# Weight conversion in two VectorE passes, one operation for sum and inverse, pairs from unit 16: one attention and gated MLP kernel, replanned

## The chip, the cores and the metric

The kernel runs on one core of one Trainium2 chip. The metric is the device time of one execution in microseconds. The median of three runs of the kernel before is 406.76 us (406.49 to 407.43).

## The reference

Attention over 4 batches, 8 heads, 768 positions and 64 columns a head, followed by a gated MLP over the joined heads. A query sees the 8 first keys and the 96 latest; the bias is a slope per head times the distance.

```python
scores = q @ k.T / sqrt(64) - slope * dist          # kept: key < 8, or 0 <= rel < 96
a = exp(scores - max);  a = a / (sum(a) + 1e-9)
x = (a @ v) heads joined                            # [4, 768, 512]
h = gelu(x @ w_in);  u, v = h[:, :512], h[:, 512:]  # w_in float64
v_n = layernorm(v) * g_ln
v_s = w_sg @ v_n + b_sg                             # mixes the 768 positions
out = x + (u * v_s) @ w_out                         # w_out float64
```

## The kernel before, in words

**Units.** Attention is cut into 48 units: batch, then the third of the queries (256 rows, two tiles), then the pair of heads (four pairs). So units 0 to 11 are batch 0, 12 to 23 batch 1, and units 16 to 19 are the middle third of batch 1. For one unit the DMA queue loads q and k (`load_qk`, L1086, 380 KB) and v (`load_v`, L1093), TensorE makes 16 small score products (`score`, L1112), VectorE adds the bias and takes the largest (L1134, four per unit), ScalarE takes the exponential with its sum (L1139, four), the four sums get 1e-9 added on the engine that the plan chooses (ScalarE L1146, GpSimd L1148, VectorE L1150), VectorE inverts them (L1152), and GpSimd scales the four blocks (L1159). Then the weights are transposed. Units 0 to 15 (`TURNS`) do it on TensorE (L1220) with a copy out of PSUM (L1225). Later units do it by VectorE in 32x32 blocks (L1188), four DMAs to DRAM (`far<-tt`, L1196) and one back (`pt<-far`, L1200). Last TensorE multiplies by v (`weigh`, L1247): 24 products, then a score step, then 8 more that add to the same banks.

**Singles and pairs.** Up to unit 19 units are weighed one by one; from unit 20 (`PAIRS`, L121) two at a time, so 48 products, scores, 16 products, and the scores run one unit further ahead. Up to unit 19 (`DIRECT`, L119) `take` (L1333) copies the result to `xh` (L1345) and splits it from there into a high and a low part of x (L1357, L1363); from unit 20 `take_late` splits it straight from PSUM (L1320, L1324), the low part on VectorE.

**The MLP** works in split float: each operand is a high part rounded for TensorE plus the rest, and a product is three (L598, L599, L600). Per batch there are six v tiles (512 columns), and u, mix and out tiles (384 columns). Batch b's MLP runs beside batch b+1's attention. The last output is made from 28 instead of 32 block products (`Blocks`, L846).

**Weights.** `w_in` and `w_out` arrive as float64. `load_split` (L922) turns a piece into float32 by integer arithmetic: ScalarE scales the high word (L937), then VectorE makes three passes: shift left by 3 (L940), or-in the low word's top bits (L942), or-in the sign (L944). A copy (L947) and a difference (L949) make the two parts. There are 20 such pieces: four of 512 columns (the v half of `w_in`, needed by the first product of the MLP), eight of 256 (the u half), eight of 256 (`w_out`). `w_sg` is float32 and needs no conversion. `w_out`'s raw piece lies in a tile of the set `t`, its result in one of the set `diag`, four tiles each; the MLP's temporaries are in `t` too.

**The order.** Nothing is queued by hand. Each operation is entered with the engines that could do it and their modelled times (`op`), a due time is worked back from TensorE's list, and each due time gets a shift from the long string `SHIFTS`. `order` (L378) then plays the plan: each engine takes, by due time plus shift, the first operation that is ready and has room. The instructions are emitted in that order and each engine keeps it. TensorE stays within 40 operations of its own list. Before 29 us it fills planned gaps with products of zeros into a bank that is about to be used (`zeros` L534, `keep_on` L542).

```python
119 DIRECT = 20
121 PAIRS = 20
537 if not n or gap < IDLE or o.begin > ON_UNTIL: return 0
```

Of the kernel before, what the change touches and what calls it, by code (L numbers as in the profile page):

```python
# [1723 lines left out]
```

## Time and profile before

| | |
|---|---|
| median of 3 runs | 406.76 us |
| the profiled execution's own time | 408.85 us |
| its span, first to last instruction | 407.1 us |
| TensorE, VectorE, ScalarE, GpSimd busy | 97, 77, 56, 57% of the span |
| DMA | 68.78 MB, mean 169 GB/s |

The span is what the trace covers; 1.75 us of the profiled execution lie around it. The profiled execution is 2.09 us above the median. Busy TensorE is not TensorE at its peak: the ends of products are modelled, and products of zeros count as busy.

### The profile page before, as it was taken

Reading aid. Unit: us, or ns where it says so; the run is one execution under the profiler, and the core shown is the slowest. Engines: PE = TensorE matmul, PEld = TensorE weight load, DVE = VectorE, ACT = ScalarE, POOL = GpSimd, SP = SyncE. Lnnn points to the kernel's source line nnn. Section 1 sums busy time; section 2 is a strip of 40 time slices with the busy share of each in tenths; the row PEclk is TensorE's granted clock in tenths of the full one; section 3 lists DMA queues with packets and bytes.
Section 4 is the critical chain, followed back from the end, with each engine's and each line's share of the span. In section 5 each row is a group of like instructions: output and inputs, shape, how many; then the busy total and the mean of one; then the engine's idle time right before and its main releaser. Section 6 shows DMA issues by size and latency. Waiting matters only on the chain.

```text
span 407.1 us, 11302 instructions
## 1 busy us (share of the span) xinstructions
PE 395.3 (97%) x3980; PEld 358.5 (88%) x3980; DVE 312.0 (77%) x1041; ACT 226.1 (56%) x746; POOL 233.2 (57%) x395
## 2 busy tenths in 40 slices
PE   7989999999988999999999999999999999999994
PEld 4878778999977888999999898999999888999994
DVE  5897999999968889967766889957766668823782
ACT  5999999956637556544244575644245244533310
POOL 3766976673857566373455536354455244899640
PEclk9999999999999999999999999999999999999999
DMA  7866756148799696747778784746657521000004
GB/s 216 317 191 184 241 196 209 55 161 252 184 288 298 193 289 187 198 120 205 185 245 237 224 232 124 209 99 204 184 206 195 163 61 39 2 1 0 2 22 142
DMA packets 50368, 68.78 MB, mean 169 GB/s; under 512 B 5888, under 2 KB 34432, under 8 KB 50304
## 3 DMA queue, kind: packets, MB, share of 16 engines
q1 hardware_dynamic: 50304, 67.99, 56.2%
q8 instruction: 33, 0.54, 0.6%
q14 instruction: 31, 0.25, 0.2%
HBM read 49.61 MB, written 18.35 MB: 167 GB/s over the span
## 4 chain that ended last, share of the span: by engine, by line
PE 80%; DVE 8%; DMA 5%; SPq 2%; POOL 1%; issue 1%; ACT 0%; DVEq 0%; ACTq 0%
PE mm_ps L598 21%; PE mm_ps L600 20%; PE mm_ps L599 20%; PE av L1247 7%; PE s_ps L1112 6%; PE mm_ps L846 4%; PE tps L1220 3%; DMA qk<-in_qk_in_dram 3%; DMA far<-tt 2%; SPq L1196 1%; DVE p L1134 1%; POOL p L1159 1%; DMA v<-in_v_in_dram 1%; DVE tt L1188 1%; DVE win L949 1%
## 5 line engine op out<-in xcount | busy, mean ns | idle before, releaser
L1139 ACT ACTIVATE p<-p,pst 128x168 f32<-128x168 f32 (+1 forms) x192 | 81.2, 429 | 34.6 <-DVE pst L1134 32.6
L1159 POOL TENSOR_SCALAR p<-p,pst 128x168 f32<-128x168 f32 (+1 forms) x187 | 84.5, 469 | 24.0 <-DVE pst L1152 22.3
L598 PE MATMUL mm_ps<-wsg,z 128*128 128x384 f32 x192 | 64.9, 338 | 0.0
L600 PE MATMUL mm_ps<-wsg,z 128*128 128x384 f32 x192 | 64.2, 334 | 0.0
L599 PE MATMUL mm_ps<-wsg,z 128*128 128x384 f32 x192 | 64.2, 334 | 0.0
L1134 DVE CUSTOM_DVE_ANT_0 p<-s_ps,bias 128x168 f32<-128x168 f32 (+1 forms) x192 | 53.1, 317 | 6.0 <-PE s_ps L1112 4.0
L1247 PE MATMUL av<-pt,v 64*64 64x128 f32 (+1 forms) x1408 | 48.9, 250 | 1.9 <-DVE pst L1152 1.1
L1247 PEld LDWEIGHTS av<-pt,v 64*64 64x64 f32 x1408 | 40.6, 133 | 10.6 <-issue 3.8
L598 PE MATMUL mm_ps<-x,win 128*128 128x384 f32 x128 | 43.7, 342 | 0.0
L600 PE MATMUL mm_ps<-x,win 128*128 128x384 f32 x128 | 42.9, 335 | 0.2 <-DVE win L949 0.2
L599 PE MATMUL mm_ps<-x,win 128*128 128x384 f32 x128 | 42.8, 334 | 0.0
L1112 PE MATMUL s_ps<-qk 64*64 64x168 f32 (+1 forms) x768 | 38.7, 307 | 2.0 <-DMA qk<-in_qk_in_dram 2.0
L598 PE MATMUL mm_ps<-win,x 128*128 128x512 f32 x96 | 39.7, 413 | 0.0
L714 POOL TENSOR_TENSOR o<-o,x 128x384 f32<-128x384 f32 x24 | 24.3, 1016 | 25.4 <-DVE o L712 16.0
L1188 DVE STREAM_TRANSPOSE tt<-p 128x384 f32<-128x384 f32 (+1 forms) x64 | 33.4, 545 | 7.0 <-POOL p L1159 3.6
L600 PE MATMUL mm_ps<-win,x 128*128 128x512 f32 x96 | 37.7, 393 | 0.0
L599 PE MATMUL mm_ps<-win,x 128*128 128x512 f32 x96 | 37.7, 392 | 0.0
L1139 ACT ACTIVATION_READ_ACCUMULATOR p<-p,pst 128x1 f32 x192 | 37.5, 195 | 0.0
L598 PEld LDWEIGHTS mm_ps<-wsg,z 128*128 128x128 f32 x192 | 36.0, 188 | 1.1 <-issue 0.9
L1148 POOL TENSOR_SCALAR pst<-pst 128x4 f32<-128x4 f32 x38 | 9.9, 260 | 46.5 <-ACT p L1139 43.3
L600 PEld LDWEIGHTS mm_ps<-wsg,z 128*128 128x128 f32 x192 | 36.0, 188 | 0.1
L599 PEld LDWEIGHTS mm_ps<-wsg,z 128*128 128x128 f32 x192 | 36.0, 188 | 0.0
(148 smaller groups left out, 926.4 us busy)
## 6 DMA issues: line engine op xcount, KB each, us to landing
qk<-in_qk_in_dram SPq DMA_DIRECT2D x32, 380.0 KB, 4.2
far<-tt SPq DMA_DIRECT2D x96, 96.0 KB, 2.4
pt<-far SPq DMA_DIRECT2D x24, 384.0 KB, 4.6
v<-in_v_in_dram SPq DMA_DIRECT2D x32, 256.0 KB, 3.9
out_dram<-o SPq DMA_DIRECT2D x28, 192.0 KB, 2.8
qk<-in_qk_in_dram SPq DMA_DIRECT2D x15, 276.0 KB, 3.5
v<-in_v_in_dram SPq DMA_DIRECT2D x16, 192.0 KB, 3.2
far<-tt SPq DMA_DIRECT2D x32, 80.0 KB, 2.9
```

The source lines that it names most:

```text
L598: mm(ps.ap, ah, bh, start=(i == 0), stop=False)
L599: mm(ps.ap, ah, bl, start=False, stop=False)
L600: mm(ps.ap, al, bh, start=False, stop=(i == n - 1))
L714: lo = lambda eng: eng.tensor_tensor(o.ap, o.ap, xm[:, 1, :].bitcast(F32), ALU.add)
L846: mm(ps.ap, pa(h)[:, ms], pb(g), start=(first and k == n == 0), stop=True, skip_group_check=True)
L1112: nc.tensor.matmul(to, qk[rows, qc:qc + HQ], keys, start=True, stop=True)
L1134: nc.vector.tensor_tensor_reduce(out=p[:, g, 0:nk], in0=s_ps[h][:, i * W:i * W + nk], in1=bias[:, 2 * j + h, w0:w0 + nk], op0=ALU.add, op1 ...
L1139: op([on_act(nk, 0.225) + (lambda p=p, g=g, nk=nk, i=i: nc.scalar.activation(p[:, g, 0:nk], p[:, g, 0:nk], AF.Exp, bias=st[:, 0, i, g:g + ...
L1159: op([on_pool_ts(nk, -0.10) + (partial(scaled, lambda o, a, c: nc.gpsimd.tensor_scalar(o, a, c, 1.0, ALU.mult, ALU.mult)),),][:1 if n < TU ...
L1188: nc.vector.transpose(out, src.rearrange("p g (b j) -> p g b j", j=QB))
L1220: nc.tensor.transpose(tps[i][:, a * P:(a + 1) * P], pc[:, c:c + P], ident)
L1247: nc.tensor.matmul(to, v[rows, vc:vc + D], of, stop=True, skip_group_check=True, **kw)
```

## The change

- **Conversion.** The shift left and the sign no longer have passes of their own on VectorE. One pass multiplies the high word as a float by 0.0, which leaves its sign alone, in place in the raw piece, on GpSimd or on VectorE as the plan chooses (`SIGN` = 999 lets both be chosen). Then VectorE ors the low word's top bits into that, and a second VectorE pass shifts the scaled word left by 3 and ors it in.
- **Sum and inverse** are one operation of the plan: on VectorE the two instructions in a row, or on GpSimd an addition and a power of -1 (`POWER` = 0 lets both be chosen). ScalarE no longer takes part.
- **Pairs** and the direct split of x begin at unit 16 instead of 20 (`PAIRS`, `DIRECT`).
- **Tiles.** The set `diag` is gone, `t` has six tiles instead of four, and both tiles of a `w_out` piece come from `t`.
- **Zeros.** The first operation on a bank that is planned to begin between 5 and 9 us gets four products of zeros ahead of it if it had none (`WARM`).
- **Model and order.** The played plan adds 0.9 us once to the first DMA after 2.4 us (`STALL`), one rule of the order changes from 7.773 to 7.178, and all 62-base shifts are new.

```diff
-RULES = (7.773165816547267, 15.003852384881524, 0.25509251116156784)
+RULES = (7.177642220784175, 15.003852384881524, 0.25509251116156784)
 SHIFTS = (
...
-DIRECT = 20
+DIRECT = 16
-PAIRS = 20
+PAIRS = 16
-PLACES = {..., "pst": 2, "diag": 4, "tt": 1, ..., "t": 4, ...}
+PLACES = {..., "pst": 2, "tt": 1, ..., "t": 6, ...}
+STALL = 2.4, 0.9
+SIGN = 999
+LOW = 999
+POWER = 0
+WARM = 5.0, 9.0, 4
...
                     wire = max(wire, t + 1.3) + way[2]
+                    if t > STALL[0] and not stalled:
+                        wire, stalled = wire + STALL[1], True
...
-        for _ in range(o.zeros):
+        more = WARM[2] if n and WARM[0] < o.begin < WARM[1] else 0
+        for _ in range(o.zeros or more):
...
-        op([("DVE_SB", 0.07 + n / 1850, 0.15 + n / 1850, lambda: nc.vector.tensor_scalar(
-            a(), a(), 3, None, ALU.logical_shift_left))], [], [f])
+        signs = lambda eng: eng.tensor_scalar(words()[:, :, 1].bitcast(F32),
+                                              words()[:, :, 1].bitcast(F32), 0.0, None, ALU.mult)
+        op([on_pool_ts(n) + (partial(signs, nc.gpsimd),),
+            on_dve_sb(n, 0.02) + (partial(signs, nc.vector),)][:1 if n >= SIGN else 2], [f], [raw])
         op([on_dve_sb(n, 0.02) + (lambda: nc.vector.scalar_tensor_tensor(
-            a(), words()[:, :, 0], 29, a(), ALU.logical_shift_right, ALU.bitwise_or),)], [raw], [f])
+            words()[:, :, 1], words()[:, :, 0], 29, words()[:, :, 1], ALU.logical_shift_right,
+            ALU.bitwise_or),)], [], [raw])
         op([on_dve_sb(n, 0.02) + (lambda: nc.vector.scalar_tensor_tensor(
-            a(), words()[:, :, 1], -0x80000000, a(), ALU.bitwise_and, ALU.bitwise_or),)],
-           [raw], [f])
+            a(), a(), 3, words()[:, :, 1], ALU.logical_shift_left, ALU.bitwise_or),)], [raw], [f])
...
-        op([on_act(4, 0.13) + (lambda: nc.scalar.activation(
-            sums(1), sums(1), AF.Identity, bias=w.tiny),),
-            ("POOL_TS", 0.24, 0.28, lambda: nc.gpsimd.tensor_scalar(
-                sums(1), sums(1), 1e-9, None, ALU.add)),
-            ("DVE", 0.13, 0.20, lambda: nc.vector.tensor_scalar(
-                sums(1), sums(1), 1e-9, None, ALU.add))], [], [st])
-        op([("DVE", 0.19, 0.28, lambda: nc.vector.reciprocal(sums(2), sums(1)))], [], [st])
+        def inverse():
+            nc.vector.tensor_scalar(sums(1), sums(1), 1e-9, None, ALU.add)
+            nc.vector.reciprocal(sums(2), sums(1))
+        def power():
+            nc.gpsimd.tensor_scalar(sums(1), sums(1), 1e-9, None, ALU.add)
+            nc.gpsimd.tensor_tensor(sums(2), sums(1), w.minus.to_broadcast([P, 4]), ALU.pow)
+        op([("POOL_TS", 0.84, 0.88, power), ("DVE", 0.32, 0.40, inverse)][:1 if n < POWER else 2], [], [st])
...
-                Buf(lambda i: ap.tile([P, 4 * HQ], F32, tag=f"diag{i}", name="stage")[:, 0:n], "diag"))
+                Buf(lambda i: tp.tile([P, FF], F32, tag=f"t{i}", name="stage")[:, 0:n], "t"))
```

## Rows read from the trace of the kernel before

**Rows 1.** The first part of the page: busy time, share of the span and number of instructions of each engine over the whole profiled execution.

```profile
PE 395.3 (97%) x3980; PEld 358.5 (88%) x3980; DVE 312.0 (77%) x1041; ACT 226.1 (56%) x746; POOL 233.2 (57%) x395
```

**Rows 2.** Busy time by stage: length of the stage, then busy microseconds (and instructions) of each engine, the granted TensorE clock, the DMA engines' mean share and GB/s. The stages: the first scores; up to the first product of batch 0's first layer; that layer's v half beside attention; the rest of the weight conversions; units 16 to 19; from there to the last product.

```profile
5.00:10.00 5.00, 4.18 (x60) 2.89 (x60) 3.21 (x25) 4.16 (x19) 1.26 (x4) 1.00 0.94 305
10.00:30.00 20.00, 18.64 (x319) 15.27 (x317) 18.20 (x74) 19.06 (x72) 14.04 (x28) 1.00 0.77 259
30.00:66.00 36.00, 35.84 (x510) 27.04 (x508) 31.97 (x138) 35.23 (x132) 26.43 (x51) 1.00 0.64 199
66.00:100.00 34.00, 33.83 (x283) 31.96 (x286) 33.24 (x101) 25.17 (x75) 22.09 (x34) 1.00 0.57 175
100.00:133.00 33.00, 30.67 (x354) 28.18 (x347) 26.60 (x99) 21.29 (x80) 23.36 (x38) 1.00 0.84 247
133.00:401.00 268.00, 268.00 (x2457) 251.33 (x2456) 195.49 (x595) 119.70 (x370) 143.91 (x227) 1.00 0.51 148
```

**Rows 3.** The waits of TensorE over the whole span: who waited for whom, us in total, times, longest.

```profile
PE s_ps L1112 <- DMA qk<-in_qk_in_dram: 2.0, 2, 1.2
...
PE av L1247 <- DVE pst L1152: 1.1, 1, 1.1
PE tps L1220 <- POOL p L1159: 0.7, 2, 0.4
...
PE mm_ps L600 <- DVE win L949: 0.2, 1, 0.2
```

**Rows 4.** The timeline of TensorE's first products: start, us, engine, line, operation, tiles and shape, count. L547 are the zeros, L1112 the scores.

```profile
1.24 3.82 PE L547 MATMUL s_ps<-bsg 128*128 128x336 bf16 x13 [1.24 <-DVE bsg L982]
4.99 1.76 PE L1112 MATMUL s_ps<-qk 64*64 64x128 f32 x32
7.57 0.73 PE L1112 MATMUL s_ps<-qk 64*64 64x128 f32 x16 [0.82 <-DMA qk<-in_qk_in_dram]
8.24 2.45 PE L547 MATMUL tps<-bsg 128*128 128x384 bf16 x14
```

**Rows 5.** The timeline of ScalarE near the start: the fifth of its exponentials, which is the first of unit 1.

```profile
8.25 0.42 ACT L1139 ACTIVATE p<-p,pst 128x168 f32<-128x168 f32 x1
```

**Rows 6.** The table by stage for the zeros (L547) alone: TensorE busy (and products), its weight loads, clock, DMA share, GB/s.

```profile
10.00:30.00 20.00, 5.36 (x74) 4.47 (x71) 1.00 0.77 259
```

**Rows 7.** VectorE's groups by line and shape: busy us in total, mean ns of one, idle time just before them and what ended it. L940, L942: two of the three passes of a conversion; L1150, L1152: sum and reciprocal.

```profile
L1152 DVE RECIPROCAL pst<-pst 128x4 f32<-128x4 f32 x48 | 7.9, 169 | 9.7 <-POOL pst L1148 8.0 <-ACT pst L1146 1.4
...
L940 DVE TENSOR_SCALAR stage<-stage 128x256 int32<-128x256 int32 x16 | 5.4, 339 | 0.0
...
L942 DVE SCALAR_TENSOR_TENSOR stage<-stage 128x512 int32<-128x512 int32 x4 | 2.8, 702 | 0.1
...
L940 DVE TENSOR_SCALAR stage<-stage 128x512 int32<-128x512 int32 x4 | 1.7, 421 | 0.2 <-ACT stage L937 0.2
L1150 DVE TENSOR_SCALAR pst<-pst 128x4 f32<-128x4 f32 x3 | 1.3, 447 | 1.0 <-ACT p L1139 0.9
```

**Rows 8.** The same view of GpSimd: L1159 is the scaling of the softmax, L1148 the sum plus 1e-9, L659 the power -0.5 of the layer norm.

```profile
L1159 POOL TENSOR_SCALAR p<-p,pst 128x168 f32<-128x168 f32 x155 | 70.5, 469 | 21.0 <-DVE pst L1152 19.7 <-PE tps L1220 0.5 <-DVE xh L1346 0.4
...
L1159 POOL TENSOR_SCALAR p<-p,pst 128x128 f32<-128x128 f32 x32 | 14.6, 468 | 3.0 <-DVE pst L1152 2.5 <-DVE xh L1346 0.4
...
L659 POOL TENSOR_TENSOR rs<-rs,small 128x1 f32<-128x1 f32 x24 | 13.7, 572 | 12.4 <-DVE rs L656 12.0
...
L1148 POOL TENSOR_SCALAR pst<-pst 128x4 f32<-128x4 f32 x38 | 9.9, 260 | 46.5 <-ACT p L1139 43.3 <-ACT xh L1345 1.6 <-POOL o L714 0.4
```

**Rows 9.** The same view of ScalarE: L1225 evacuates transposed weights of attention, L1146 is the sum plus 1e-9.

```profile
L1225 ACT COPY pt<-tps 128x384 f32<-128x384 f32 x23 | 10.7, 486 | 0.5 <-PE tps L1220 0.5
...
L1146 ACT ACTIVATE pst<-pst,small 128x4 f32<-128x4 f32 x7 | 2.1, 295 | 0.1
```

**Rows 10.** The waits of VectorE between 5 and 66 us.

```profile
DVE pst L1152 <- ACT pst L1146: 1.4, 2, 0.8
...
DVE pst L1152 <- POOL pst L1148: 1.0, 2, 0.5
DVE pst L1150 <- ACT p L1139: 0.9, 1, 0.9
```

**Rows 11.** GpSimd's timeline between 100 and 150 us: four scalings of one unit each time.

```profile
102.82 3.18 POOL L1159 TENSOR_SCALAR p<-p,pst 128x168 f32<-128x168 f32 x4
...
119.28 1.56 POOL L1159 TENSOR_SCALAR p<-p,pst 128x168 f32<-128x168 f32 x4 [0.31 <-DVE pst L1152]
```

**Rows 12.** VectorE's timeline between 102 and 121 us, beside and behind those two times four.

```profile
103.39 0.42 DVE L942 SCALAR_TENSOR_TENSOR stage<-stage 128x256 int32<-128x256 int32 x1
...
120.87 0.58 DVE L1188 STREAM_TRANSPOSE tt<-p 128x384 f32<-128x384 f32 x1 [1.68 <-POOL p L1159]
```

**Rows 13.** The timeline of SyncE between 100 and 150 us, which issues every DMA: one load of transposed weights back (L1200), and the loads of two units' q and k (L1086).

```profile
114.55 0.33 SPq L1200 DMA_DIRECT2D pt<-far  x1
...
125.81 0.93 SPq L1086 DMA_DIRECT2D qk<-in_qk_in_dram  x2
```

**Rows 14.** TensorE's timeline between 116 and 133 us: the two products before which it stood.

```profile
119.32 0.68 PE L1247 MATMUL av<-pt,v 64*64 64x128 f32 x24 [1.06 <-DVE pst L1152]
...
131.40 0.73 PE L1112 MATMUL s_ps<-qk 64*64 64x128 f32 x16 [1.18 <-DMA qk<-in_qk_in_dram]
```

**Rows 15.** From the answer on the loads back of transposed weights (L1200): time from issue to landing.

```profile
DMA to landing us min/median/max: 3.0/4.5/6.2
```

More of the change, by code (lines that the diff above doesn't have):

```diff
@@ new lines @@
+    "aTTXtgILwl1NbI2Ffp003mEuLjctI3fHlkxD0N00PdiKhvBBoN00002xxDiu00AvgWzwmP5JGsY6b1E700hP6FakksHU1NgbISR3"
+    "XoWozki7qEKV43Efdb0000TY00NB6QAHzwNc00cE3tGbOP00lxaCeNhHgTzwFgJdH3BFB16HIMHEyJ6qVbUMiHslOJ8sUUHMTDCs"
+    "HvXkjvXbWiGWSLBvM915ENyOXhuymEoJX28v5KSFDXKCgsizYGsslcNiQaNxOG3OxoyoUqy8gpzcN0yuzc3EnooCw5ICT1F9fxN0"
+    "H3zAzwmA4VwqRGi0DWwAHgpmzwR5JlkVhJRlWWys1P9jDpxS9wPrdwueqIwbHBjeHwXQbn1iGNTJkvYVzAzFrEzYy1zwdNzwmHQs"
+    "vqRfQKmjUGE48WzwrEucEixKZDfJu9zwltkVFU2WzwGRswcNrC6nl6MBmlzwlxzQVDITfKBQmDn2kP8u4JqTuesYSssNNszQuyzQ"
@@ new lines @@
+    "zQLsLmahm3pKsVQCt4vznBpxzQygzQsdefCCy3zQzQJWM62T2TLe754v4zPzpUp4pu4u2zAgiLElq93HrKt2cC2fOzArVH3el9CP"
+    "BH8KdrlhEJAe2zB1OUSAG82zy5VQ2zGqoc2zOkdWy0gYDMSP5Onyf9zwjXXTvJskQQzwzwK3UZzwm7zwrbfIwMLOcQgN3P3PcXK6"
+    "3R726e495dbQJ3WslN00JbNW00nIzwJ0vpRo6M8eT7rlzw8InhoOzwrhwFatzwqwHrcjzwmfzw3PZuzwzwrjbMzwqIcjzwFFzwtK"
+    "49WQUxGSJR5Ad9IfsMngPg2nfJOcaKN5rorI7FGF3PbiQypemXzwId9UaSxzYbm6h5zwzwgYsLfkzwvVvDvYY0uBzwHERtlHwcj9"
+    "vczwD1custkmzwhevczwS7zwj1q1qQQmXoNPzw4lHBvUPv2WrFfqnszwzwwgwFefzwgRzwrjFcMhSyUfzwp1zwgoUBjHZRASPkGa"
@@ new lines @@
+    "WGzlGPQhf5zwzw5DNuV4UXzwKGz5g1o3zwPwLH3wQzr2FxCpraYhQkr1YCe5t4AxVoCyvpmTXejaQ5Qy2wDGZu2wYqGvlrdj2wCI"
+    "sBoFDIsS6Oz3fRVvN4YM4PJnCfsihgOD3jZN3ezujUdR4dN2cj4U4cYY8bBpJAa1h5KCER2w2WBpMWWOGgG4Fdb8WvzwP04C00C2"
+    "O2RZ00SsyltPFrAGN85Ik75aCQlm4CC7FdvqJl9AAdrmNowxPRtVqRud77GJ4V32rjMepnNeJkBU00iVzwJB004ZU0jsITUrDlAG"
+    "HYkF000G8PA3leg6MRhKsMkegyjwqAbfzEWQve00iIwYL5YLzw5o0000GqABzwQ3QTQiM1Ql00ad90FuiEPyzwzwf2vzeQWuuO1m"
+    "CJbjJJmoH5SvsAYQdhzwhWWV0DPhHZ6eD2Hn1m1mS6ufcFhdzwhOzw4QmjDSiPngUlBGyVcxzenPs0bMWVi33zH7AXzwJU5wi0zw"
@@ new lines @@
+    "zweno9fw1CTCzwooNz5ZzwPkTZeJ4OFQzwG2sxb6CSzwenCIS3BcLXEn3SO3b700zwOAzwAVzJc3HU9u7PGEzwxMZqzw5n98cEtd"
+    "180WxrUPFf00Hx00h7LolBQXajCBys4u65sh41H4ZdEWGvfFQkdW00nJI6oRsvRXGM1ifohs52Tbz9jszwivyikSviVzcCjuYlFk"
+    "BNS4ye5xalzR00XtqXkHCrHIpDzw9y9yJzPazwnDQ1H0AZkF9yvN9yHrVofN9y9yzw2z5o000nm0BcOaLZ1R3B8JUCvgzw21NJ7E"
+    "CnEQBwfd5IBb4jDRK17y3uC61uWu3YCb0rct3CX5Pszw00003AUkFs6iqD0000SL00PfPU5i0000WmEt43ceFcr7LhZ4PlfT7qn0"
+    "oKOciO6i6aFfS3004q3p74NWzw4gPRBW242KFW4Q4Ech2hL172Jj2qSZFu1RDBGz6cWXJXHnaW00VrMKbhEGRCE694o3ZAYblK6V"
@@ L107 @@
+    "8F2Q81Mc00zw6LxgD0RxrV0fY200zwH2YgVx1C00zwgYzHXpMj0000jU1N25sccJb0bF00GtiEYBnVlSzw"
 )
@@ L117 @@
 TURN = 0.105
-DIRECT = 20
-PAIRS = 20
+DIRECT = 16
+PAIRS = 16
 Q4 = 4
 QB = P // Q4
-PLACES = {"qk": 3, "v": 2, "p": 4, "pst": 2, "diag": 4, "tt": 1, "far": 3, "pt": 2, "xh": 2, "x": 11, "z": NT, "gt": KD + 1,
-          "t": 4, "st": 2, "mv": 2, "rs": 2, "bank": 8}
+PLACES = {"qk": 3, "v": 2, "p": 4, "pst": 2, "tt": 1, "far": 3, "pt": 2, "xh": 2, "x": 11, "z": NT, "gt": KD + 1,
+          "t": 6, "st": 2, "mv": 2, "rs": 2, "bank": 8}
 def unit_widths(u):
```

91 lines of the change are left out of this document (34 added, 57 removed).

## The prediction

> **What bounds the kernel now.** I read the page's first part, then busy time by stage, then TensorE's waits, and only then single lines. The page says TensorE is busy 395.3 of 407.1 us [rows 1], so at first sight it alone is the bound. The stages say where that is true. From 133 to 401 us it is busy 268.00 of 268 us, and from 30 to 100 it lacks 0.33 us [rows 2]; its one wait for another engine there is the 0.2 us before a product that needs a weight difference [rows 3]. No change of another engine can gain there. Two stages differ.
>
> From 10 to 30 us ScalarE is busy 19.06 of 20 us, VectorE 18.20, GpSimd 14.04 [rows 2]; TensorE's 18.64 include 5.36 of zeros [rows 6]. Here the softmax of the first units and the first weight conversions are the bound, ScalarE first and VectorE close behind. When TensorE gets its first dense work is decided here, and what is gained here moves everything behind it.
>
> From 100 to 133 us every engine has room, but TensorE misses 2.33 us [rows 2]. The waits are two: 1.06 us before a v product at 119.32 and 1.18 us before scores at 131.40 [rows 14]. The first is put down to a reciprocal that was long done; the load back of that unit's weights was issued at 114.55 [rows 13], lands after 4.5 us in the median [rows 15], at about 119.1, and fits. The second is a q and k load issued from 125.81 on [rows 13]. The DMA engines are 84% busy in that stage [rows 2]. So this is DMA latency.
>
> **The change part by part.** The sum stands against the profiled execution's own 408.85 us (span 407.1 and 1.75 around it); the result is then carried to the median by 406.76/408.85. A measurement of this kernel can tell about 0.2%, 0.8 us, from no change.
>
> *Conversion.* The removed pass is L940: 0.421 us at 512 columns, four times, and 0.339 us at 256, sixteen times [rows 7], 7.1 us of VectorE. The passes that stay are the dearer kind (0.702 at 512). The new sign pass is in no row. On VectorE it costs from 0.421 (the pass it replaces, also one source) to 0.702 (L942): nothing gained, up to 1.1 us lost over the four large pieces. On GpSimd VectorE is rid of 4 x 0.421 = 1.7 us before 30 us. I take GpSimd for the large pieces, because that stage has 5.96 us of GpSimd idle and 1.80 of VectorE [rows 2]. ScalarE is the fuller engine and loses nothing itself, so a freed VectorE microsecond is worth half: a 0.486 us copy of transposed weights [rows 9] can move over and both then end together. That is -0.85 us, with 0 and -1.7 as ends. The eight pieces of the u half free 2.7 us between 30 and 66 us, where TensorE has 0.16 us to give [rows 2]: -0.1. The eight of `w_out` fall into stages where TensorE is full: 0, covered by its own products; without that cover they would bring 2.7 us.
>
> *Sum and inverse.* VectorE's reciprocal waits 8.0 us for GpSimd's and 1.4 for ScalarE's sum over the whole run [rows 7]; between 5 and 66 us it is 1.4 + 1.0 + 0.9 = 3.3 us [rows 10]. The pair of instructions on one engine has no handover, and ScalarE is rid of 0.295 us a time [rows 9]. VectorE gets an addition for it, of at least about a reciprocal's 0.169 us [rows 7]. About a third of the 3.3 us lies before 30 us by length of time; less the additions and halved as above, -0.2 us, with 0 and -1.1 as ends. On GpSimd the operation is 0.260 (L1148) plus at least 0.572 (the power, L659) [rows 8], 0.83 us in place of 0.26.
>
> *Pairs and direct split from 16.* Four single visits become two double ones. A double visit waits for both units' weights, behind it stand all of TensorE's MLP products of batch 0, since TensorE keeps its order, and x of batch 1 waits for the visit. On the DMA queue the q and k loads of one more unit go ahead of the loads back; two such issues take 0.93 us [rows 13], so each delays a load back by about 0.47. The two v loads of a pair go together. But everything after 133 us is run in pairs and TensorE misses nothing there [rows 2], and the scores run a unit further ahead of need. Ends: -2.24 us (both waits go) and, since a second unit's load could now end the wait twice, +1.06 more for each of two pairs. I take half the waits, -1.1, as the busy DMA engines stay as busy. What is late next is the load back again. The direct split takes eight 128-column copies off ScalarE and puts the low parts on VectorE; neither is full between 100 and 133 us (21.29 and 26.60 of 33): 0.
>
> *Zeros.* Thirteen products of 336 columns take 3.75 us up to 4.99, 0.288 us each; fourteen of 384 at 8.24 take 2.45 us, 0.175 each, half as much per column, so the first run at the 1.2 GHz level and the later at 2.4 [rows 4]; the granted clock is 1.00 from 5 us on [rows 2]. Four more ahead of the scores of units 1 and 2 cost up to 1.15 us each. TensorE waits 0.82 us for unit 2 anyway, and ScalarE comes to unit 1 only at 8.25 [rows 4, 5], 1.5 us after its scores end at 6.75. Cost 0, covered by ScalarE's queue; at worst 2.3 - 0.8 = 1.5 us.
>
> *Tiles, model, order.* Six tiles in `t` hold what eight in two sets held while `w_out` loads, and free two for the MLP later; TensorE is full there, 0. New shifts can move 0.2 us here and there in either direction; within the full stages I count 0.
>
> Sum: -0.85 - 0.1 - 0.2 - 1.1 = -2.25, so 406.6 against 408.85, and 404.5 us at the median. Its own range, 403.0 to 405.9, is where the start or the pairs give all or nothing.
>
> **A rule against the trace.** Four scalings took 1.56 us while VectorE stood still for 1.68, and 3.18 beside conversion passes [rows 11, 12]. The Trainium skill (SBUF — State Buffer, Who interferes with whom) says that a VectorE instruction with two SBUF inputs and a GpSimd one that reads SBUF exclude each other for the whole instruction; the trace agrees as far as a doubling. By that rule the sign passes on GpSimd would pay it every time, since the two passes left on VectorE have two inputs; the first rival carries the price.
>
> **The rivals.**
>
> *GpSimd becomes the bound of the start (slower).* In proportion to columns, a sign pass of 512 costs from 1.19 us (1.56/4 for 168 columns) to 2.4 (3.18/4) [rows 11], four of them 4.8 to 9.7. Powers add 0.57 for each of about six units (14.04 us busy hold at most seven times four scalings), 3.4. Together 8.2 to 13.1 against 5.96 us idle: from 5.96 on it decides. The scalings (0.469 each [rows 8]) queue behind, and the transposes wait for them, as they do twice already [rows 3]. The middle, 4.7 us over, less VectorE's 1.80 idle that can take some back, less 1.1 from the pairs: +1.8, 408.5 us. For it: the doubling above. Against: both new operations may go to VectorE.
>
> *The start gives everything (faster still).* Freed time is refilled from ScalarE in full and both DMA waits go: -1.7 - 1.1 - 0.16 - 2.24 = -5.2, 401.6 us. For it: the passes and handovers sit in the fullest stage. Against: ScalarE's exponentials cannot move.
>
> *Little changes.* The sign pass stays on VectorE, so there are still three passes, ScalarE holds the start, and the pairs trade one DMA wait for another: -0.4, 406.4 us. For it: 84% DMA. Against: 9.7 us of idle before the reciprocal alone.
>
> **How the numbers follow.** Forecast 0.42, GpSimd-bound 0.22, everything 0.18, little 0.18. Faster by over 0.2% (below 405.95): 0.42 + 0.18 + a little of the last, 0.62; slower (above 407.57): 0.22; between: 0.16. The range runs from 401.6, the larger gain, to 408.5, the GpSimd case; it leaves out halves of these two cases, about 0.2.
>
> **What would show it.** Right: L940's group gone from VectorE and a sign group of four 512-column passes on GpSimd; fewer zeros than 5.36 us between 10 and 30 us, waits of TensorE between 100 and 133 us about halved; no idle before the reciprocal. Wrong: GpSimd over 19 of 20 us between 10 and 30 us with transposes waiting for scalings; the two DMA waits as long under other names; or TensorE's stage after 133 us no longer full, which would mean that the new order and not these steps sets the time.

## The result and the profile after

The changed kernel is slower: 412.56 us in the median of six runs beside 407.10 for the kernel before, a ratio of 1.0115 with a 95% interval of 1.0076 to 1.0153, so 4.7 us by the ratio, which this text goes by. The forecast was 404.5 us, 401.6 to 408.5; the result lies outside it. The profiled execution took 412.31 us, close to its median; its span is 410.5. That of the kernel before took 408.85 us, 1.75 above the 407.10, so the two traces differ by 3.4 us only.

The first part of the page and the table by stage (length, busy us and instructions of PE, PEld, DVE, ACT, POOL, then clock, DMA share, GB/s) answer to [rows 1] and [rows 2]:

```profile
PE 397.1 (97%) x3978; PEld 358.3 (87%) x3978; DVE 311.0 (76%) x1007; ACT 223.3 (54%) x736; POOL 278.2 (68%) x431
```

```profile
5.00:10.00 5.00, 5.00 (x60) 3.12 (x63) 3.65 (x26) 4.42 (x19) 0.94 (x3) 1.00 0.84 266
10.00:30.00 20.00, 17.67 (x314) 13.62 (x315) 18.29 (x70) 17.78 (x67) 14.14 (x23) 1.00 0.77 250
30.00:66.00 36.00, 35.53 (x506) 27.31 (x507) 32.14 (x141) 34.56 (x128) 29.20 (x54) 1.00 0.68 209
66.00:100.00 34.00, 32.47 (x299) 29.45 (x292) 31.73 (x88) 25.23 (x79) 28.26 (x38) 1.00 0.46 143
100.00:133.00 33.00, 32.19 (x329) 30.37 (x327) 27.55 (x97) 19.20 (x67) 27.13 (x42) 1.00 0.87 258
133.00:401.00 268.00, 267.14 (x2460) 249.67 (x2459) 192.59 (x571) 120.58 (x379) 176.39 (x258) 1.00 0.52 149
```

GpSimd works 45 us more. TensorE has new gaps: it misses 2.33 us from 10 to 30 (1.36 before), 1.53 from 66 to 100 (0.17 before), 0.86 behind 133 (none before). Behind 10 us it misses less only from 100 to 133, 0.81 for 2.33. The waits of TensorE name the partner; they answer to [rows 3]:

```profile
PE tps L1235 <- POOL p L1174: 2.6, 6, 0.8
PE s_ps L558 <- DVE bsg L995: 1.2, 1, 1.2
PE av L1262 <- DMA pt<-far: 0.8, 1, 0.8
PE mm_ps L611 <- POOL wout L962: 0.7, 1, 0.7
PE mm_ps L609 <- DVE pst L1160: 0.5, 1, 0.5
```

Transposes wait 2.6 us for scalings (L1174, the old L1159) where it was 0.7, and a product waits for GpSimd's weight difference (L962). The same view from 5 to 30 us has 2.0 of the 2.6:

```profile
PE tps L1235 <- POOL p L1174: 2.0, 4, 0.8
```

Five of the six waits stand ahead of the first power of the run, which starts at 67.78 us; the sixth, at 71.93, is 0.38 us. The waits for q and k are gone; that of unit 2 is filled with zeros. Now GpSimd's groups by line and shape (busy us, mean ns | idle before), beside [rows 8]:

```profile
L1165 POOL TENSOR_TENSOR pst<-pst,small 128x4 f32<-128x4 f32 x32 | 33.7, 1054 | 2.7
...
L951 POOL TENSOR_SCALAR stage<-stage 128x256 f32<-128x256 f32 x11 | 10.2, 933 | 0.2 <-ACT stage L948 0.2
L1164 POOL TENSOR_SCALAR pst<-pst 128x4 f32<-128x4 f32 x32 | 9.1, 285 | 37.4 <-ACT p L1152 34.9 <-PE av L1262 1.4
```

Every unit from 16 on takes its inverse there, by an addition (L1164) and a power (L1165): 1.34 us together, where the planner holds 0.84. A sign pass of 256 columns (L951) takes 0.93 us. Those two groups are 43.9 of the 45 us. On VectorE the same view, beside [rows 7]:

```profile
L955 DVE SCALAR_TENSOR_TENSOR stage<-stage 128x512 int32<-128x512 int32 x4 | 3.0, 743 | 0.0
L958 DVE SCALAR_TENSOR_TENSOR stage<-stage 128x512 int32<-128x512 int32 x4 | 2.9, 726 | 0.0
...
L951 DVE TENSOR_SCALAR stage<-stage 128x512 f32<-128x512 f32 x4 | 1.9, 479 | 0.3 <-ACT stage L948 0.2
```

The four large pieces of `w_in` keep three passes on VectorE; their sign passes did not go to GpSimd. Last the start of TensorE, which answers to [rows 4]:

```profile
5.78 0.74 PE L558 MATMUL s_ps<-bsg 128*128 128x336 bf16 x4
6.45 0.73 PE L1125 MATMUL s_ps<-qk 64*64 64x128 f32 x16
7.12 2.88 PE L558 MATMUL s_ps<-bsg 128*128 128x336 bf16 x19
9.93 0.73 PE L1125 MATMUL s_ps<-qk 64*64 64x128 f32 x16
...
30.02 0.48 PE L609 MATMUL mm_ps<-win,x 128*128 128x512 f32 x1
```

Unit 2's scores begin at 9.93 instead of 7.57, and the first MLP product at 30.02 instead of 27.44, where it stands before:

```profile
27.44 0.50 PE L598 MATMUL mm_ps<-win,x 128*128 128x512 f32 x1
```

The traces below bear that out. In the four of the order before (conversion, power, and inverse alone, late TensorE) the product begins between 27.01 and 27.68 us. In the six of the changed kernel's order whose softmax and conversion are whole up to 30 us it begins between 29.68 and 31.43.

Below, "lag" is a figure worked out from two traces: the moment at which TensorE has done the same amount of products (zeros left out, each kind at its shortest time), minus that of the kernel before. For the changed kernel it is 1.7 us at 30 us, 0.5 at 69, 4.7 at 111, 1.8 from 136 to 245 and 2.95 from 286 to the end. Between 69 and 136 part of it is only another order of attention and MLP products. It counts from an execution of the kernel before that was itself 1.75 us over the median. One execution's lag can be off by half a microsecond through the first loads; around 30 us, where the kinds of products stand in another order, it also hangs on the shortest times taken (1.0 to 2.5 us in place of the 1.7), so the start is read from the first MLP product below.

### The profile page after: what moved, and what is told of

Same layout as the page of the kernel before. It is cut to its first block, busy times and chain, and to the rows that moved or that the text cites. A ratio compares the mean times of both kernels' runs of the same rounds, so it can differ in the third digit from the quotient of the medians.

```text
span 410.5 us, 11264 instructions
## 1 busy us (share of the span) xinstructions
PE 397.1 (97%) x3978; PEld 358.3 (87%) x3978; DVE 311.0 (76%) x1007; ACT 223.3 (54%) x736; POOL 278.2 (68%) x431
## 4 chain that ended last, share of the span: by engine, by line
PE 72%; DVE 12%; POOL 5%; DMA 4%; ACT 3%; issue 2%; SPq 1%; DVEq 0%; POOLq 0%; ACTq 0%
PE mm_ps L609 19%; PE mm_ps L611 18%; PE mm_ps L610 18%; PE av L1262 6%; PE s_ps L1125 5%; PE mm_ps L857 4%; POOL p L1174 3%; DVE p L1147 2%; DMA pt<-far 2%; DMA far<-tt 2%; ACT p L1152 1%; PE tps L1235 1%; PE s_ps L558 1%; DVE vg L628 1%; DVE tt L1203 1%
## 5 line engine op out<-in xcount | busy, mean ns | idle before, releaser
L1152 ACT ACTIVATE p<-p,pst 128x168 f32<-128x168 f32 (+1 forms) x192 | 80.8, 425 | 38.2 <-DVE pst L1147 35.8
L1174 POOL TENSOR_SCALAR p<-p,pst 128x168 f32<-128x168 f32 (+1 forms) x186 | 82.5, 461 | 17.8 <-DVE pst L1161 7.2
L1262 PE MATMUL av<-pt,v 64*64 64x128 f32 (+1 forms) x1408 | 46.9, 250 | 1.4 <-DMA pt<-far 0.8
L1262 PEld LDWEIGHTS av<-pt,v 64*64 64x64 f32 x1408 | 39.5, 133 | 9.2 <-issue 4.0
L1152 ACT ACTIVATION_READ_ACCUMULATOR p<-p,pst 128x1 f32 x192 | 36.8, 192 | 0.0
L1165 POOL TENSOR_TENSOR pst<-pst,small 128x4 f32<-128x4 f32 x32 | 33.7, 1054 | 2.7
```

The lines of the kernel that those rows point to most:

```text
L1152: op([on_act(nk, 0.225) + (lambda p=p, g=g, nk=nk, i=i: nc.scalar.activation(p[:, g, 0:nk], p[:, g, 0:nk], AF.Exp, bias=st[:, 0, i, g:g + ...
L1165: nc.gpsimd.tensor_tensor(sums(2), sums(1), w.minus.to_broadcast([P, 4]), ALU.pow)
L1174: op([on_pool_ts(nk, -0.10) + (partial(scaled, lambda o, a, c: nc.gpsimd.tensor_scalar(o, a, c, 1.0, ALU.mult, ALU.mult)),),][:1 if n < TU ...
L1262: nc.tensor.matmul(to, v[rows, vc:vc + D], of, stop=True, skip_group_check=True, **kw)
```

## The experiments

"Changed" is the changed kernel with its order kept, "before" the kernel before with its order kept, unless a new search is named. In most of them the instructions alone differ and not the places in the queues. Ratios are to the kernel before, run on the same chip; what one kernel gains over another is the difference of their ratios, times 407 us. Edits are shortened to what matters, and `SHIFTS` and `RULES` of orders searched anew are left out.

**A cheap power.** Changed; the power on one column.

```diff
-nc.gpsimd.tensor_scalar(sums(1), sums(1), 1e-9, None, ALU.add)
-nc.gpsimd.tensor_tensor(sums(2), sums(1), w.minus.to_broadcast([P, 4]), ALU.pow)
+nc.gpsimd.tensor_scalar(sums(2), sums(1), 1e-9, None, ALU.add)
+nc.gpsimd.tensor_tensor(sums(2)[:, 0:1], sums(2)[:, 0:1], w.minus, ALU.pow)
```

> The changed kernel with the order of all instructions kept; GpSimd's power is taken on 1 of the 4 columns (the addition writes the other three into the result, so three of four inverses of the units from 16 on are left out). Its duration should fall from the 1.05 us of the trace to near the 0.57 us that a power of one column took before. Theory A (operations on GpSimd take longer than the order was made for, so that scalings, transposes and TensorE behind them are late): 1 to 2 us less than the changed kernel's 412.6, and the lag that it gains between 70 and 111 us and at 251 us becomes smaller. Theory B (the loads and zeros of the first 20 us, and the order as such, cost the time): within 0.3 us of the changed kernel. Theory C (GpSimd is the bound of the start, the rival of the prediction): no change, since no power runs before 66 us.

409.30 us, 1.0052 (1.0033 to 1.0072): 0.63% back, about 2.6 us. The group of the power:

```profile
L1165 POOL TENSOR_TENSOR pst<-pst,small 128x1 f32<-128x1 f32 x32 | 18.7, 584 | 2.7
```

Half a microsecond less, 32 times, is worth half of the loss. The wait for a load back at 252.85 (0.84 us) is gone with it, and the lag behind 266 us is 1.3 instead of 2.95. That wait is absent without the added zeros too, where the powers are whole, but there the lag still grows by 1.1 us between 245 and 286 us, before other products; with the cheap power it does not grow. The transposes' waits for scalings stay at 2.5 us. So theory A is right in its direction, with more than its 1 to 2 us, and not in the transposes that it named.

**Shorter sign passes.** Changed; on GpSimd 192 of 256 columns.

```diff
-signs(nc.gpsimd)                      # words()[:, :, 1]
+signs on words()[:, 0:3 * n // 4, 1]  # on GpSimd only
```

> The changed kernel with the order kept; GpSimd's eleven sign passes cover 192 of their 256 columns (a quarter of the signs of those weight pieces is left out), so that each should take about 0.70 us in place of 0.93. Theory A: 0.5 to 2 us less, with a smaller gain of lag between 70 and 100 us, where five of these passes run. Theory B: within 0.3 us of the changed kernel. Theory C: within 0.3 us as well, since the sign passes of the first 30 us are on VectorE in the trace.

410.69 us, 1.0073 (1.0045 to 1.0101); the intervals overlap with the changed kernel's, the middle is 1.7 us lower. The pass takes 804 ns, not the 700 expected:

```profile
L953 POOL TENSOR_SCALAR stage<-stage 128x192 f32<-128x192 f32 x11 | 8.8, 804 | 0.3 <-ACT stage L948 0.2
```

So eleven passes shorter by 0.13 us come with 1.7 us in the middle, more than the 1.4 us that they hold. Suggestive, not settled.

**No added zeros.** Changed.

```diff
-WARM = 5.0, 9.0, 4
+WARM = 5.0, 9.0, 0
```

> The changed kernel without the four zero products ahead of the scores of the first units, everything else in the same order. Theory A: within 0.3 us. Theory B, as far as it is the zeros: 0.4 to 0.7 us less, the 0.67 us that the four take before 6.45 us in the trace. As the prediction had it (covered by ScalarE's queue): within 0.2 us. Should the lower granted clock come back in the first 10 us without them: 0.3 to 1 us more.

412.32 us, 1.0124 (1.0094 to 1.0154). No difference.

**The first loads as before.** Changed.

```diff
+# unit 2's q and k issued ahead of the first w_in piece;
+# 0 instead of 19 zeros ahead of its scores, 14 behind them
```

> The changed kernel with one exchange in the queue of loads, as it stood in the kernel before: the q and k of unit 2 are issued ahead of the first piece of w_in, and the 19 zero products that bridged the wait for them stand, 14 of them, behind its scores. Everything else in the same order. Theory B (the new order of the first loads makes unit 2 late, and all of the start behind it): 1 to 1.9 us less than the changed kernel, with unit 2's scores at about 7.6 us in place of 9.9 and the lag of the start gone to half or less. Theory A: within 0.3 us, since the start is not where the wrong durations are. Theory C: within 0.3 us, as GpSimd's work in the start is the same.

412.16 us, 1.0121 (1.0089 to 1.0153). Unit 2's scores moved to 7.28 us as expected, but the first MLP product only from 30.02 to 29.68. Theory B falls: TensorE had been waiting for something later anyway.

**Three edits together.** Changed, with the cheap power, the shorter sign passes and the first loads.

> The changed kernel in its own order with three edits together: power on 1 of 4 columns, GpSimd's sign passes on three quarters of their columns (the rest of both is left out), and unit 2's q and k ahead of the first w_in piece. Alone they measured 409.3, 410.7 and 412.2 us against the 412.6 of the changed kernel. Theory A (durations on GpSimd that the order did not hold): the first two add up, 3.3 and 1.9 us less, so about 407.4 us, the time of the kernel before. If both only free the same stretch of TensorE: about 409 us. Of the pairs: if the two load waits between 100 and 133 us are gone only because TensorE comes there late, they come back here by as much as the lag at 111 us shrinks; if the pairs removed them, they stay gone.

409.79 us, 1.0067 (1.0051 to 1.0084): no more than the cheap power alone. The edits do not add. TensorE is full behind 133 us again (268.00 of 268). The lag at 111 us stayed at 4.6, so this kernel said nothing on the pairs.

**Inverse on VectorE everywhere.** Changed.

```diff
-("POOL_TS", 0.84, 0.88, power)
+("POOL_TS", 0.84, 0.88, inverse)   # same place in the order, both instructions on VectorE
```

> The changed kernel in its own order, with the sum and inverse of the units from 16 on also on VectorE (addition and reciprocal) in place of GpSimd's addition and power; nothing is left out. Theory A: GpSimd is rid of 32 times 1.34 us and VectorE gets 32 times about 0.35, so 2.5 to 4 us less than the changed kernel, 408.5 to 410 us. If a handover from VectorE to GpSimd or VectorE's own queue costs as much as the power: within 0.5 us of 412.6.

411.09 us, 1.0098 (1.0077 to 1.0119). Expected 408.5 to 410. That is 0.17% back, with intervals that overlap, beside the 0.63% of the cheap power. VectorE is not a free place for it either.

**The conversion alone.** Before, with the three new passes in the places of the old.

```diff
-a() <<= 3;  a() |= low >> 29;  a() |= high & 0x80000000
+high = 0.0 * high;  high |= low >> 29;  a() = (a() << 3) | high
```

> The kernel before in its own order, with the three passes of the new conversion in the places of the three old ones, all on VectorE. By the durations in the trace after (479 + 726 + 743 ns for 512 columns in place of 421 + 702 + 702) four large pieces cost 0.5 us more, the sixteen small ones 16 times about 0.05. Theory A: +0.2 to +0.6 us, as VectorE is not the fullest engine of the start. If the dearer passes make the lag of the start (1.7 us at 30 us): +1.2 to +1.9 us. If the change's conversion is cheaper anywhere: -0.2 us or less.

407.33 us, 1.0009 (0.9993 to 1.0025). No difference that can be measured, with all three passes on VectorE.

**The power alone.** Before.

```diff
-op([("DVE", 0.19, 0.28, lambda: nc.vector.reciprocal(sums(2), sums(1)))], [], [st])
+op([("DVE", 0.19, 0.28, inverse)], [], [st])  # reciprocal for n < 16, else GpSimd's power
```

> The kernel before in its own order, where from unit 16 on the inverse of the sums is GpSimd's power in place of VectorE's reciprocal; nothing is left out. About 1.05 us on GpSimd 32 times. Theory A: 2 to 4 us more than the kernel before, 409 to 411 us, with transposes waiting for scalings between 66 and 133 us. If only the new order is to blame and GpSimd has room: within 0.4 us.

412.51 us, 1.0140 (1.0120 to 1.0160): 5.7 us slower, more than expected and more than the whole change. The power's group and TensorE's waits (the first is as before):

```profile
L1158 POOL TENSOR_TENSOR pst<-pst,small 128x4 f32<-128x4 f32 x32 | 33.7, 1052 | 1.5
```

```profile
PE s_ps L547 <- DVE bsg L984: 1.3, 1, 1.3
PE av L1255 <- POOLq L1285: 1.1, 2, 0.9
PE av L1255 <- ACTq L1285: 1.0, 1, 1.0
PE tps L1228 <- POOL p L1167: 0.9, 3, 0.4
```

```profile
133.00:401.00 268.00, 265.35 (x2434) 246.95 (x2433) 192.02 (x569) 120.53 (x372) 171.67 (x255) 1.00 0.51 144
```

TensorE misses 2.65 us behind 133 us (busy 265.35 of 268), where the kernel before missed nothing. Before a visit's last products it waits for GpSimd's and ScalarE's queues: L1285 is an empty instruction that the planner puts on one of three engines behind a visit's first products, and the last ones wait for it. That it comes late on GpSimd fits the powers in that queue; why ScalarE's, where no power runs, comes late is open. The transposes' waits of 0.9 us all lie before 30 us; between 66 and 133 us, where theory A put them, there are none.

**The start: large sign passes left out.** Changed.

```diff
-partial(signs, nc.vector)
+partial(signs, nc.vector) if n < 512 else (lambda: None)
```

> The changed kernel in its own order without the sign passes of the four 512-column pieces of w_in, which VectorE makes in the first 30 us (four times 0.48 us; these signs are left out). Theory V (VectorE's queue holds the start of the changed kernel): 1 to 1.7 us less than its 412.5, and the lag of 1.7 us at 30 us becomes 0.5 or less. Theory G (the scalings on GpSimd hold it): 0 to 0.5 us less, as far as scalings beside VectorE's passes become shorter. Theory O (the first loads and the order itself): within 0.3 us.

411.58 us, 1.0088 (1.0056 to 1.0120): 1.1 us less by the ratio, which is in theory V's range and over theory G's, but the intervals overlap. The first MLP product begins at 29.48 us instead of 30.02, so most of the 2.6 us of the start stay, where theory V had a lag of 0.5 or less. From 5 to 30 us transposes wait for scalings 0.7 us in two waits, instead of 2.0 in four. Theory V falls short of the start; that the passes have a part in it is possible.

**The start: half scalings.** Changed.

```diff
-put(ps[i][:, g, 0:nk], ps[i][:, g, 0:nk], st[:, 2, i, g:g + 1])
+c = nk // 2 if n < 6 else nk
+put(ps[i][:, g, 0:c], ps[i][:, g, 0:c], st[:, 2, i, g:g + 1])
```

> The changed kernel in its own order, the scalings of the first six units on half of their columns (the other half stays unscaled). In the trace after these 24 scalings are 8.3 us of the chain in the first 30 us. Theory G: 1 to 2 us less than 412.5, the lag at 30 us 0.5 or less. Theory V: 0 to 0.5 us less. Theory O: within 0.3 us.

410.47 us, 1.0078 (1.0048 to 1.0108), about 1.5 us less, with overlapping intervals again. The trace, of the fastest of seven runs (409.04), begins the first MLP product at 28.32 us instead of 30.02, and no lag is left at 30 us. Scalings on GpSimd from 5 to 30 us, first in the changed kernel, then in this one:

```profile
5.00:30.00 25.00, 14.11 (x24) 1.00 0.78 254
```

```profile
5.00:30.00 25.00, 11.47 (x24) 1.00 0.82 267
```

Half the columns save only 2.6 of 14.1 us, and TensorE's first MLP product comes 1.7 us earlier, outside all other traces of the changed kernel's order. The transposes' waits for scalings from 5 to 30 us fall from 2.0 us to 0.5. Theory G fits: GpSimd's scalings are on the path there, though GpSimd is busy only 14.14 of 20 us from 10 to 30; of its idle time in the changed kernel's start 6.4 us end with an inverse. The edit leaves out work, so it shows the path and not how much of the loss arises there.

**Sum and inverse on VectorE alone.** Before, all units.

```diff
-# sum on ScalarE, GpSimd or VectorE, then reciprocal on VectorE
+nc.vector.tensor_scalar(sums(1), sums(1), 1e-9, None, ALU.add)
+nc.vector.reciprocal(sums(2), sums(1))       # at the reciprocal's place
```

> The kernel before in its own order, where the addition of 1e-9 stands on VectorE right ahead of the reciprocal in every unit and no longer on GpSimd or ScalarE; nothing is left out. The prediction's step: -0.2 us, with 0 and -1.1 as ends. If the handover behind VectorE's addition only moves and VectorE is late by 48 more small instructions: up to +0.5 us.

410.08 us, 1.0061 (1.0040 to 1.0083): 2.5 us slower instead of 0.2 faster. VectorE's two groups, which answer to the first and last of [rows 7]:

```profile
L1147 DVE TENSOR_SCALAR pst<-pst 128x4 f32<-128x4 f32 x48 | 11.6, 242 | 5.3 <-ACT p L1139 5.0
L1148 DVE RECIPROCAL pst<-pst 128x4 f32<-128x4 f32 x48 | 8.5, 178 | 1.6
```

The reciprocal's 9.7 us of idle time became 1.6, but 5.3 of it stand ahead of the addition now, since VectorE waits for ScalarE's sum itself. So 3.8 us of waiting are won (9.7 and 1.0 in [rows 7] against 5.3 and 1.6) and 10.9 us of work added (20.1 against 9.2 for both groups), all in VectorE's queue. That this balance is the 2.5 us is argued and not shown: the trace is of the fastest of twelve runs (408.78 us), no slower than that of the kernel before, and so cannot show where a median run loses them.

**A late TensorE.** Before, with 26 zero products ahead of two MLP products.

```diff
+for o in scores[:2]: o.zeros = 13   # the first two operations on a bank behind 85 us
```

> The kernel before in its own order, with 26 added zero products on TensorE, 13 each ahead of two MLP products near 92 us (about 4.6 us by the 0.175 us of such a product), so that TensorE comes to the stage of 100 to 133 us as late as in the changed kernel (lag 4.7 us at 111 us). It is a test of what removed the two load waits there. Theory P (the pairs from unit 16 removed them): this kernel has no such pairs, so both waits stay as far as loads and scores keep their distance, and the time is about 4 to 4.6 us more than before. Theory L (lateness alone: the loads are issued by other engines' progress and are there when TensorE comes): the waits of 1.06 and 1.18 us vanish, the lag falls back by about 2.2 us, and the time is 2 to 2.6 us more.

412.21 us, 1.0114 (1.0081 to 1.0146), 4.6 us more. In its trace the added products cost 4.3 us of lag, of which 2.9 are left at 136 us. The two waits of [rows 14]:

```profile
122.92 0.68 PE L1255 MATMUL av<-pt,v 64*64 64x128 f32 x24 [0.92 <-DMA pt<-far]
133.90 0.73 PE L1120 MATMUL s_ps<-qk 64*64 64x128 f32 x16 [0.35 <-DMA qk<-in_qk_in_dram]
```

The wait for the load back stays, that for q and k shrinks by 0.83 us, and the median kept all 4.6 us, as theory P has it. But neither wait is a fixed property of the order before. The conversion alone, with that order, no new pairs and no lateness (the traced execution took 406.86 us), has 0.59 us at the first and nothing at the second, where the scores begin at 129.31 us; TensorE misses 0.86 of the 33 us and not 2.33:

```profile
118.26 0.68 PE L1248 MATMUL av<-pt,v 64*64 64x128 f32 x24 [0.59 <-DVE pst L1153]
100.00:133.00 33.00, 32.14 (x339) 29.35 (x332) 26.74 (x99) 21.09 (x78) 23.53 (x40) 1.00 0.86 250
```

With the power alone TensorE has neither, and with sum and inverse on VectorE none near 119 us and 0.55 us near 131. So the waits change from trace to trace where order and pairs stay, and what removed them in the changed kernel is not settled by these runs.

**The pairs alone.** Before, direct split and pairs from 16, the order searched anew from the old shifts (less search than the two kernels had).

```diff
-DIRECT = 20
+DIRECT = 16
-PAIRS = 20
+PAIRS = 16
```

> The kernel before with one part of the change alone, direct split and pairs from unit 16 on, and the shifts of the order searched anew from those of before (with less search than the two kernels had). Nothing is left out. The prediction's step: -1.1 us, with -2.24 and +1.06 as ends, so about 406; the waits of TensorE for the load back near 119 us and for q and k near 131 us gone or halved. If the pairs do nothing, or a new order takes away what they give: 407 to 409 us, with waits elsewhere.

408.19 us, 1.0019 (1.0003 to 1.0035). TensorE misses 0.19 us from 100 to 133 (busy 32.81 of 33) instead of 2.33, but behind that stage it waits at the next visit, for the load back again:

```profile
149.58 0.63 PE L1246 MATMUL av<-pt,v 64*64 64x128 f32 x21 [1.04 <-DMA pt<-far]
150.53 0.68 PE L1246 MATMUL av<-pt,v 64*64 64x128 f32 x24 [0.26 <-DMA pt<-far]
```

The lag is -0.95 us at 136 us and about +0.7 from 156 on. So in this execution TensorE was ahead and lost it at the next visit, in this order. Since the waits before are not steady, one trace does not show that the pairs won it; the median shows no gain.

**All but the power, order searched anew.**

```diff
-op([("POOL_TS", 0.84, 0.88, power), ("DVE", 0.32, 0.40, inverse)][:1 if n < POWER else 2], [], [st])
+op([("DVE", 0.32, 0.40, inverse)], [], [st])
```

> The changed kernel with sum and inverse on VectorE in all units, and the order searched anew for that. Nothing is left out. In the changed kernel's own order this measured 411.1 us. If the work of the power on GpSimd and an order made for it were the loss: 407 to 409 us. If the rest of the change (conversion, fused inverse on VectorE, start) costs its part whatever the order: 410 to 411 us, about the 2.3 us that the fused inverse cost in the order before.

410.08 us, 1.0072 (1.0054 to 1.0089), inside the second expectation and near what the fused inverse on VectorE cost in the order before (1.0061). So the power is not the whole loss: without any, 2.9 us are left. That they are the fused inverse's here too is not shown; half a microsecond lies outside the span, around which this kernel has 2.3 us where the others have 1.8.

**Measured durations in the planner, order searched anew.**

```diff
-("POOL_TS", 0.84, 0.88, power)
+("POOL_TS", 1.34, 1.38, power)
-on_pool_ts(n) + (partial(signs, nc.gpsimd),)
+('POOL_TS', 0.05+n/290, 0.09+n/290) + (partial(signs, nc.gpsimd),)
```

> The changed kernel with two durations in its planner set to the trace's (1.34 us in place of 0.84 for addition and power on GpSimd, 0.93 in place of 0.71 for a sign pass of 256 columns) and the order searched anew for them; the power stays on GpSimd. Nothing is left out. If the wrong durations in the order are the loss: 409 to 410 us. If the power's work is a burden in any order: 411 to 413 us.

410.92 us, 1.0096 (1.0074 to 1.0117), at the border of the two expectations and inside the changed kernel's interval. Transposes still wait:

```profile
PE tps L1235 <- POOL p L1174: 3.5, 6, 1.2
```

All six waits stand ahead of this kernel's first power, at 83.51 us, so they say nothing of it. The wrong durations are at most a small part. Between this kernel and the one without the power, each with an order of its own, lies 1.0 us, and the intervals overlap. How far a longer search would bring either is not known. No version here beats the kernel before.

## Why the prediction was wrong

**Sum and inverse: the step that failed.** It stood in the sum at -0.2 us with 0 and -1.1 as ends, no loss allowed. Alone it measured +2.5 us with both instructions on VectorE and +5.7 us with the power on GpSimd from unit 16 on, each in the order before; and in the changed kernel a cheap power gave back 2.6 of the 4.7 us. Two things were missed. The step named the GpSimd price ("0.260 plus at least 0.572, 0.83 us in place of 0.26") and then put no term on it: 32 units times that difference is 18 us of GpSimd, and it had room only in the average. And 0.572 us was the price of one column. Four columns take 1.054, so the true difference is 1.08 us a unit, 35 us for 32 units, in the queue in which the scalings stand. How it reaches TensorE differs: through empty instructions and other late operations in the power alone, between 245 and 286 us in the changed kernel; hardly through TensorE's transposes, 78 of whose 88 products the changed kernel makes before the first power. On VectorE the forecast counted the handover as won; the trace shows a part of the idle time moved ahead of the addition.

**Conversion.** -0.95 us was forecast; with all three passes on VectorE 0.0 (+0.09%) was measured. The sum took GpSimd for the four large sign passes, as it had idle time on average; they stayed on VectorE, so the start still has three passes there, as the rival "little changes" had it. Eleven passes of 256 columns went to GpSimd, behind 53 us, where the sum counted 0.1 us or nothing; what they cost there is not settled.

**Pairs.** The term took half of two waits that stood in one execution, 2.09 us slower than the median, as a steady cost. In the trace of the conversion alone, in the same order and near the median (406.86 us), 0.59 of their 2.24 us is left; so there may have been little to win. Both waits went in the changed kernel and in the one with the pairs alone, but by what is not shown. Alone the time did not fall: in its trace the load back is late at 150 us instead, as the step said ("what is late next is the load back again") without a price. -1.1 us in the sum against +0.2%.

**Zeros.** Right: cost 0, measured 412.32 without them beside 412.56 with. Zeros from 10 to 30 us are 5.25 us busy beside 5.36 [rows 6].

**Order.** Counted as 0 with 0.2 us here and there. The first loads did change place and no price of it could be measured (1.0121 beside 1.0115); what the new order as a whole gives or takes was not measured. The prediction's sign for an order that sets the time, a stage after 133 us that is no longer full, came (267.14 of 268). But with the order kept and the power made cheap it was full again in two traces, so this order does not by itself break it.

**The rival "GpSimd becomes the bound of the start"** had the side right, with 408.5 us, and not the place: GpSimd is busy 14.14 of 20 us there, no large sign pass runs on it, and the powers run only behind 66 us. What it shares with the outcome is a sign that it named: transposes that wait for scalings in the start, 2.0 us instead of 0.7, and a start that comes earlier with half scalings. The loss by the power, behind 66 us, is not of that kind.

Added up, the parts alone give more than the whole: 5.7 for the power, nothing for the conversion, some 0.8 for pairs, and a third of 2.5 for the 16 units inverted on VectorE, 7.3 against 4.7 measured. Each was measured in an order without the rest, and the three edits together showed that effects do not add here; so the sum proves nothing on the new order. Of the late start (30.02 instead of 27.44 us) it is shown only that GpSimd's scalings are on its path; which instruction ahead of them makes them late is open, and so is whether VectorE's sign passes have a part.

## What to carry to other kernels

An operation that moves to an engine with idle time is paid at that engine's own price times its count, and in its queue: put the product in the sum even where the engine's average is low. A price from another shape is a lower end, not a price; ask for an upper one. A wait that one slow execution shows is not yet a cost: look for it in a second trace of the same order before a term of the sum rests on it. And a handover removed by letting the busier engine do both steps can move the wait to that engine instead of ending it.

## What the runs showed of the hardware

GpSimd's power grows with the columns even at four: 0.584 us for one column (the cheap power), 1.054 for four (the changed kernel), so by an estimate from these two about 0.16 a column above some 0.43. VectorE's reciprocal of four columns takes 0.178 in the changed kernel. The Trainium skill (Perfetto Trace Analysis, Optimizing GPSIMD Operations) says to prefer other engines where possible, as a programmable engine is generally slower; this trace agrees, at six times for this pair of operations.

A multiplication with one input in place, on every other word, takes GpSimd 0.933 us for 256 columns and 0.804 for 192, and VectorE 0.329 for 256 and 0.479 for 512. The Trainium skill (GPSIMD Engine Reference, Engine selection) calls operations with one input roughly line-rate on GpSimd. Here GpSimd takes 2.8 times VectorE's time, and the measurement decides; but these passes run beside VectorE's work (busy 31.73 of 34 us from 66 to 100), and none was measured alone.

The first 24 scalings on half of their columns (16 of 84 instead of 168, 8 of 64 instead of 128) take 11.47 us instead of 14.11, 19% less. So most of a scaling's time there, beside VectorE's work, does not go with its columns.
